# Second turn of a decode kernel: wo turned inside the norm, w1's second half turned tile by tile, last writes on two queues, the gradient row by two transposes

## The chip, the cores and the metric

The kernel runs on one core of one Trainium2 chip. TensorE is called PE, VectorE DVE, ScalarE ACT, GpSimd POOL, SyncE SP. DMAs are issued by SP (loads, and a few writes) and by POOL (most writes), and run on 16 DMA engines.

The metric is the device time of one execution in microseconds. It is compared by medians of runs; the profile is of one execution, whose own time and span are given with it. Times inside the profile count from the start of its span.

## The reference, cut to what matters

Two layers are run with the same weights, each a decode step of attention over a cache and an MLP, and then the gradients of everything:

```python
B, Sq, D = 2, 1, 1024
Hq, Hkv, Sk, Dh = 32, 4, 16384, 128        # F = 3584
x = A_x
x = x + A(layernorm(x), k_cache, v_cache, wq, wo)      # layer 0: q = x@wq, scores over 16384 keys, softmax, @v, @wo
x = x + gelu(layernorm(x) @ w1 + b1) @ w2 + b2
x = x + A(layernorm(x), k_cache, v_cache, wq, wo)      # layer 1: the same weights and the same cache
x = x + gelu(layernorm(x) @ w1 + b1) @ w2 + b2
out, vjp = jax.vjp(f, A_x, A_k_cache, A_v_cache, A_wq, A_wo, B_w1, B_b1, B_w2, B_b2)
return (out, *vjp(grad_out))
```

All arrays are bf16. out_0 is the result, [2, 1, 1024]; out_1 the gradient of x, of the same shape; out_2 and out_3 are the gradients of the two caches, as large as these (32 MB each); out_4 to out_9 those of the weights and biases.

## The kernel before, in words

**Order of the work.** The phases are: attention forward of layer 0, its MLP, attention forward of layer 1 (to about 409 us), the *second turn* (the MLP of layer 1 forward up to the gelu and, at once, its backward, 409 to 448), attention backward of layer 1 (448 to about 640), the turn of layer 0, attention backward of layer 0, in which nearly all gradients are written, and the last writes (to 1107).

Every phase is written as a list of small pieces: `emit(fn, uses)` records a function and the chunks of memory that it uses. Nothing is scheduled by the compiler: `Program.run` calls the recorded functions one after another, so that each engine's instructions have just the order in which the pieces were emitted.

**Loads.** A `Chunk` is 1 MB, [128, 4096] bf16. There are 16 slots of that size, and some more in tiles that are free for a time (two in `e1`, two in `ds1`, one in `late`). `run` hands slots to loads in the order of first use, and issues a load on SP as early in the program as a slot will come free; on the chip, SP then waits for the last reader of that slot, and everything behind that load on SP waits too. At most 8 of SP's DMAs are in flight (8 semaphores in turn). `keep` lets a chunk that is needed again later hold its slot in between, if enough slots are left, and its second load goes away. Chunks without a load (the turned tiles of w1, the row of out_0) take slots of the same stock.

**The second turn.** w1 lies in eight tiles `ws1[j]` of [128, 3584]. The forward multiplies each with the normed x (`w1_fwd`, L862: 28 matmuls for each tile). The backward needs w1 the other way round: `turn_cols` (L470 to L476) transposes a quarter of a tile (128x448 words) on DVE into a turned tile, `w1t[h][cg]`: half h (w1 tiles 4h to 4h+3), column group cg. There are 32 such turns, at L473. `turned_products` (L479, matmuls L487) multiplies a turned tile with the gradient of the gelu's input, 28 matmuls each; that needs all four w1 tiles of its half to be turned in this column group. Sums of both halves go to `sb`, and `mlp_in_bwd` copies them out (`unquad`, L517) and takes them through the norm's backward.

The norm is `ln_fwd` (L623 to L645): two sums over partitions by PE (`part_sum`, L594), between them DVE's small steps, then the power -1/2 on POOL (L642). `mlp_in` (L913) calls it and leaves the normed x in `m_all`. The gelu is `gelu` (L881); its argument `mid` is a list of pieces run in its middle, between DVE's steps, while ACT takes the exponential.

wo, too, is turned for the first kv group of the backward: `turn_here` (L446 to L461) transposes 8 blocks of 128x128 on PE (L452) and copies them back over the original on ACT (L455). `wo_first_ops` (L969) gives eight such turns.

Before the change, `w1_turn(j)` gives the four turns of tile j. Those of tile 0 run in the end of attention forward; those of tiles 1 to 5 behind that tile's products; one turn of tile 6 in the middle of the gelu, and the other three with tile 7's four behind it. All eight turned tiles have a slot of their own. wo's turns stand two behind w1's tile 5, two behind tile 6, and four in the gelu. The products of all eight turned tiles come last (L1447 to L1488).

**The row of out_0.** The result of the MLP (`xM1`, [128, 8, 2] in f32, a column layout) is ready in the backward of layer 1, at its step 26. At step 30 (L1507) `col_to_row` (L609 to L621) turns it into two rows of 1024: eight PE transposes of [128, 2] into PSUM (L617), two copies of 2x512 on DVE (L618), and a write by POOL (L619). The row stands in a chunk of kind "load", so a later load into that slot waits on SP for the write to have landed.

**The end.** `attn_bwd` for layer 0 closes with the list at L1157 to L1161: the last units of the cache gradients (`kv_units`), the gradient of x through the first norm (`parts`; its last piece calls `col_to_row` for out_1), and the units of the last weight gradient, wq's (`units`). `pieces_rows` (L1335) with `fine` writes that gradient in 256 KB pieces, one for each 128 rows, by SP (L1349).

Of the kernel before, what the change touches and what calls it, by code (L numbers as in the profile page):

```python
# [182 lines left out]
def kernel(  # L183
# [63 lines left out]
    def flat(t):  # L247
        return t.rearrange("p a b -> p (a b)")
# [360 lines left out]
    def col_to_row(colT, dram_out, queue=None, kind="half"):  # L609
        c = P.chunk(kind=kind)  # L610

        def f():
            row = c.ap[0:2, 0:D]
            for j0 in range(0, DJ, 4):
                ps = ob()[0:2, :].rearrange("p (a b) -> p a b", a=4)
                for j in range(4):
                    PE.transpose(ps[:, j, :], colT[:, j0 + j, :], identf[:])  # L617
                V.tensor_copy(out=row[:, j0 * 128:(j0 + 4) * 128], in_=flat(ps))  # L618
            (queue or GP).dma_start(dram_out, row)  # L619

        return f, [c]  # L621

    def ln_fwd(xT, name, twice=False):  # L623
        s1 = small.tile([128, 2], F32, name="ln_s1")
        V.tensor_reduce(out=s1[:], in_=xT.rearrange("p j b -> p b j"), axis=AX.X, op=ALU.add)
        ps = part_sum(s1[:], 2)
        negmu = small.tile([128, 2], F32, name="ln_negmu")
# [7 lines left out]
        ps2 = part_sum(s2[:], 2)  # L635
        vpe = small.tile([128, 2], F32, name="ln_vpe")
# [5 lines left out]
        GP.tensor_tensor(out=rstd[:], in0=vpe[:], in1=neghalf[:], op=ALU.pow)  # L642
        y = vec.tile([128, DJ, 2], F32, name=name + "_y")
# [269 lines left out]
    def mlp_in(l, xT):  # L913
        y, r = ln_fwd(xT[:], f"m{l}", twice=True)
        V.tensor_copy(out=m_all[:, :, 2 * l:2 * l + 2], in_=y[:])
        saved[f"m{l}"] = (y, r)
# [110 lines left out]
    def attn_bwd(l, order, gT, wo_first, outputs=None, mark=None, extra=None):  # L1027
# [127 lines left out]
        if l == 1:  # L1155
            todo = tail + parts
        else:  # L1157
            rows, kv_units, units = outputs(s, True)
            todo = ev.pop(s) + kv_units[0:4] + rows + kv_units[4:6] + tail[0:4] + kv_units[6:8] + tail[4:] + kv_units[8:10]
            todo += parts[0:1] + units[0:4] + parts[1:2] + units[4:8] + parts[2:3] + kv_units[10:13] + parts[3:]  # L1160
            todo += kv_units[13:] + units[8:]  # L1161
# [173 lines left out]
    def pieces_rows(out_ap, n_in, n_out, c0=0, fine=False):  # L1335
# [302 lines left out]
```

## Time and profile before

| | |
|---|---|
| runs | 1108.69, 1110.71, 1111.01 us; median 1110.71 |
| profiled execution | 1109.68 us; its span 1107.9 us; granted PE clock 0.929 |
| busy | PE 810.2 us (73%), DVE 761.4 (69%), ACT 492.3 (44%), POOL 178.5 (16%) |
| DMA | 450.03 MB, mean 406 GB/s; SP's queue (q1) 353.41 MB, POOL's (q0) 94.43 MB |
| second turn | last V load used at 409.22, m_all at 417.70, gelu from 428.64, products' copy L517 at 439.74, first turned block of the backward (L537) at 448.07 |
| SP's waits, 420 to 520 us | 14.5 for L473 (two loads), 12.4 for out_0's row (one load) |
| out_0's row | PE from 487.85, DVE to 490.41, issued 490.71, landed 495.38 |
| end | PE, DVE and ACT done at about 1097.3; last write issued 1101.01; last DMA landed 1106.6 |

How to read it: the forty slices of the page show, for each 1/40 of the span (27.7 us), the busy share of each engine in tenths and what the DMA engines moved. Groups name an instruction by its line, engine, operation and tiles (out<-in). A wait is written as the engine and what it was about to do, then what it waited for: the total in us, how often, and the longest. "SPq" is SP's queue: SP standing before the issue of a DMA. A load counts as landed when its last part has arrived; its latency holds the time behind the loads that were issued before it.

### The profile page before, as it was taken

What the parts mean: (1) busy time and instruction counts of PE and PEld (TensorE: products, weight loads), DVE (VectorE), ACT (ScalarE), POOL (GpSimd) and SP (SyncE); (2) the same over time, 40 slices, a digit from 0 to 9 for tenths busy, and PEclk for the clock granted to TensorE, in tenths of its full rate; (3) what the DMA queues carried; (4) which work ended last, traced back from release to release, by engine and by line L of the source; (5) the groups of instructions that cost most, each with busy time, mean ns of one, the idle gap of its engine ahead of it and who ended that gap; (6) DMA issues with size and microseconds to landing.
All of it is one profiled execution on the core that took longest, in us unless ns stands there. A gap on an engine that the chain in (4) does not pass through costs nothing. (4 is left out here: it accounts for less than half of the span.)

```text
span 1107.9 us, 34190 instructions
## 1 busy us (share of the span) xinstructions
PE 810.2 (73%) x14677; PEld 608.8 (55%) x14689; DVE 761.4 (69%) x1474; ACT 492.3 (44%) x1133; POOL 178.5 (16%) x571
## 2 busy tenths in 40 slices
PE   5664666457888647888678668878886987598795
PEld 4554565456777547777677565444443444344453
DVE  5864665169888627665646475979776896598984
ACT  0322223102233222235444326777675776477874
POOL 1000000001000000111111101433332332233430
PEclk9999999999999999999878657989996998799998
DMA  9999999999999998999999989999999999999996
GB/s 375 420 423 421 421 426 421 395 403 399 418 422 422 421 421 328 409 417 421 420 421 421 417 326 406 369 381 423 420 419 425 423 420 422 425 412 420 410 423 259
DMA packets 98312, 450.03 MB, mean 406 GB/s; under 512 B 7624, under 2 KB 11734, under 8 KB 59632
## 3 DMA queue, kind: packets, MB, share of 16 engines
q1 hardware_dynamic: 81232, 353.41, 78.4%
q0 software_dynamic: 16928, 94.43, 20.7%
q8 instruction: 115, 1.88, 0.6%
q14 instruction: 37, 0.30, 0.1%
HBM read 349.20 MB, written 98.62 MB: 404 GB/s over the span
## 5 line engine op out<-in xcount | busy, mean ns | idle before, releaser
L537 DVE STREAM_TRANSPOSE kT<-slot 128x512 int32<-128x512 int32 x420 | 283.2, 694 | 109.8 <-PE sc L550 89.5
L550 PE MATMUL sc<-qbd,kT 128*128 128x32 bf16 x4096 | 262.9, 223 | 11.0 <-DVE kT L537 9.7
L550 PEld LDWEIGHTS <-kT 128*128 128x128 bf16 x4096 | 209.3, 115 | 63.7 <-issue 33.6
L575 PEld LDWEIGHTS <-slot 128*128 128x128 bf16 x3520 | 144.0, 103 | 108.6 <-issue 45.0
L575 PE MATMUL sb<-xt,slot 128*128 128x8 bf16 x3520 | 161.3, 177 | 51.1 <-DMA slot<-in_A_v_cache_dram 24.5
L276 ACT CAST slot<-sc 128x512 bf16<-128x512 f32 x293 | 166.5, 594 | 57.1 <-PE sc L1321 32.6
L1261 PE MATMUL sc<-slot,late 128*128 128x512 bf16 x345 | 128.8, 393 | 19.0 <-DVE slot L279 6.5
L279 DVE CAST slot<-sc 128x512 bf16<-128x512 f32 x170 | 113.7, 677 | 25.1 <-PE sc L1261 13.4
L763 ACT ACTIVATE e<-sc 128x512 bf16<-128x512 f32 x32 | 19.0, 597 | 235.9 <-DVE sc L760 168.3
L276 ACT CAST slot<-sb 128x512 bf16<-128x512 f32 x139 | 82.4, 593 | 38.8 <-PE sb L1321 16.9
L455 ACT COPY slot<-tp 128x512 int32<-128x512 int32 x88 | 50.2, 586 | 105.5 <-PE tp L452 105.2
L452 PE MATMUL tp<-ident,slot 128*128 128x128 bf16 x768 | 71.3, 255 | 11.9 <-DMA slot<-in_A_wq_dram 6.2
L585 ACT COPY xt<-e 32x128 int32<-32x128 int32 x256 | 75.6, 295 | 3.9
L1261 PEld LDWEIGHTS <-late 128*128 128x128 bf16 x512 | 44.5, 98 | 59.6 <-issue 46.1
L1261 PE MATMUL sb<-slot,late 128*128 128x512 bf16 x161 | 63.6, 395 | 11.7 <-DVE slot L279 6.5
L1321 PE MATMUL sc<-slot,late 128*128 128x512 bf16 x157 | 60.5, 404 | 12.3 <-DVE e L279 6.9
L437 DVE STREAM_TRANSPOSE slot<-slot 128x1024 int32<-128x1024 int32 (+1 forms) x48 | 55.3, 1177 | 16.8 <-DMA slot<-in_A_wo_dram 8.5
L452 PEld LDWEIGHTS <-slot 128*128 128x128 bf16 x768 | 57.9, 116 | 14.5 <-DMA slot<-in_A_wq_dram 6.7
L279 DVE CAST slot<-sb 128x512 bf16<-128x512 f32 x82 | 55.6, 678 | 9.2 <-PE sb L1321 3.9
L642 POOL TENSOR_TENSOR m_rstd<-ln_vpe,neghalf 128x2 f32<-128x2 f32 x2 | 1.4, 717 | 352.6 <-DVE ln_vpe L640 352.6
L585 POOL COPY xt<-late 32x64 int32<-32x64 int32 x240 | 55.2, 230 | 12.9 <-DVE late L1049 2.2
L585 POOL COPY xt<-ds 32x64 int32<-32x64 int32 x128 | 29.5, 231 | 158.6 <-DVE ds L1049 115.3
(300 smaller groups left out, 1098.7 us busy)
## 6 DMA issues: line engine op xcount, KB each, us to landing
slot<-in_A_k_cache_dram SPq DMA_DIRECT2D x105, 1024.0 KB, 17.5
slot<-in_A_v_cache_dram SPq DMA_DIRECT2D x98, 1024.0 KB, 18.0
out_dram<-slot POOLq DMA_DIRECT2D x55, 1024.0 KB, 14.4
slot<-in_A_wq_dram SPq DMA_DIRECT2D x25, 1024.0 KB, 16.1
slot<-in_A_wo_dram SPq DMA_DIRECT2D x25, 1024.0 KB, 19.7
slot<-in_B_w_dram SPq DMA_DIRECT2D x23, 896.0 KB, 15.8
out_dram<-slot POOLq DMA_DIRECT2D x40, 512.0 KB, 14.3
slot<-in_B_w_dram SPq DMA_DIRECT2D x12, 1024.0 KB, 13.5
```

What stands on the lines that cost most here:

```text
L276: S.copy(out=dst, in_=src)
L279: V.tensor_copy(out=dst, in_=src)
L437: V.transpose(out=t.ap[:, h * nw * 256:(h + 1) * nw * 256].bitcast(I32).rearrange("p (w j m) -> p w j m", j=4, m=32), in_=c.ap[:, 0:4 * nc ...
L452: PE.transpose(tp[:, j * 128:(j + 1) * 128], c.ap[:, off + j * 128:off + (j + 1) * 128], ident[:])
L455: S.copy(out=d.bitcast(I32), in_=tp.bitcast(I32))
L537: V.transpose(out=kT[:].bitcast(I32).rearrange("p (w j m) -> p w j m", w=4, j=4), in_=c.ap[:, (i % 4) * 1024:(i % 4 + 1) * 1024].bitcast(I ...
L550: PE.matmul(sc[:, a0:a0 + 4, :, 2 * (i % 4) + q], lhsT=kv[:, 2 * q + w, :, e], rhs=qbd[:, q_at(g), 2 * w + e], start=(w == 0 and e == 0), ...
L575: PE.matmul(acc, lhsT=c.ap[:, n * 128:(n + 1) * 128], rhs=xv[:, i // 4, t // 2, :, 2 * (i % 4) + t % 2], start=(fresh and i == 0 and t == ...
L585: (GP.tensor_copy if on[t % len(on)] == "g" else S.copy)(out=d[32 * t:32 * t + 32, c0:c0 + cn, j, :], in_=s[32 * j:32 * j + 32, c0:c0 + cn ...
L763: S.activation(out=e_of(l, g)[:, 8 * f:8 * f + 8].rearrange("p a h b -> p h a b"), in_=sc[f][:].rearrange("p h (a b) -> p h a b", b=8), fu ...
L1261: PE.matmul(ps, lhsT=hold["blk"][:, j, :], rhs=flat(qm(w)[:, hf * 4:hf * 4 + 4, :]), start=True, stop=True)
L1321: PE.matmul(ps, lhsT=hold[j // 4 * 4][:, j % 4, :], rhs=Y.ap[:, y_at + c0:y_at + c0 + cn], start=True, stop=True)
```

## The change

Four edits, all of them of the order and form of work that stays the same otherwise.

1. The norm of the second turn takes pieces into its three gaps (`gaps`): behind the first and the second sum, and behind the power. Into these go w1 turns 2, 3 and 4 and three of wo's eight turns; the turns ahead of the norm are two and not four. Two w1 turns stand behind each of the first six w1 tiles; two w1 turns and three of wo's turns lie in the middle of the gelu.
2. w1's second half is turned by column group, not by w1 tile: turns 16 to 19 are column group 0 of tiles 4 to 7, and so on. A turned tile of this half is then complete after four turns, and its products can follow. Products of the first half and the last two wo turns lie between. The slots: the two last turned tiles of this half take the slots of two others again, once these are read.
3. `col_to_row` makes the row of [8, 2, 128] by two transposes of [128, 8] and one copy of 8x256, and writes it in 16 pieces of 128 elements, where it had two rows of 1024. This is for out_0 and out_1.
4. The end: of the last eight 256 KB writes, those with j0 < 4 are issued by POOL, the others by SP. Two units of the cache gradients move from behind the last piece of `parts` to ahead of it.

The planner's results change with this: one V chunk more keeps its slot from the forward to the backward, so SP issues one load less.

```diff
@@ col_to_row
-            row = c.ap[0:2, 0:D]
-            for j0 in range(0, DJ, 4):
-                ps = ob()[0:2, :].rearrange("p (a b) -> p a b", a=4)
-                for j in range(4):
-                    PE.transpose(ps[:, j, :], colT[:, j0 + j, :], identf[:])
-                V.tensor_copy(out=row[:, j0 * 128:(j0 + 4) * 128], in_=flat(ps))
-            (queue or GP).dma_start(dram_out, row)
+            row = c.ap[0:DJ, 0:256].rearrange("p (b n) -> p b n", b=2)
+            ps = ob()[0:DJ, 0:256].rearrange("p (b n) -> p b n", b=2)
+            for b in range(2):
+                PE.transpose(ps[:, b, :], colT[:, :, b], identf[:])
+            V.tensor_copy(out=row, in_=ps)
+            (queue or GP).dma_start(dram_out.rearrange("b (j n) -> j b n", n=128), row)
@@ ln_fwd
-    def ln_fwd(xT, name, twice=False):
+    def ln_fwd(xT, name, twice=False, gaps=((), (), ())):
...
         ps = part_sum(s1[:], 2)
+        for fn in gaps[0]:
+            fn()
...
         ps2 = part_sum(s2[:], 2)
+        for fn in gaps[1]:
+            fn()
...
         GP.tensor_tensor(out=rstd[:], in0=vpe[:], in1=neghalf[:], op=ALU.pow)
+        for fn in gaps[2]:
+            fn()
@@ attn_bwd, the end
-            todo += parts[0:1] + units[0:4] + parts[1:2] + units[4:8] + parts[2:3] + kv_units[10:13] + parts[3:]
-            todo += kv_units[13:] + units[8:]
+            todo += parts[0:1] + units[0:4] + parts[1:2] + units[4:8] + parts[2:3] + kv_units[10:15] + parts[3:]
+            todo += kv_units[15:] + units[8:]
@@ pieces_rows
-                        nc.sync.dma_start(out_ap[(j0 + j) * 128:(j0 + j + 1) * 128, c0:c0 + cn], ap[:, j * cn:(j + 1) * cn])
+                        (GP if j0 < n_in // 256 else nc.sync).dma_start(out_ap[(j0 + j) * 128:(j0 + j + 1) * 128, c0:c0 + cn], ap[:, j * cn:(j + 1) * cn])
@@ the second turn
-    def w1_turn(j, cgs=range(4)):
-        return [turn_cols(ws1[j], j % 4, w1t[j // 4][cg], cg) for cg in cgs]
+    def w1_turn(h, j, cg):
+        return turn_cols(ws1[4 * h + j], j, w1t[h][cg], cg)
+
+    w1_turns = [w1_turn(0, j, cg) for j in range(4) for cg in range(4)]
+    w1_turns += [w1_turn(1, j, cg) for cg in range(4) for j in range(4)]
...
-    xA1 = attn_fwd(1, down, lambda: xM0, mark("e1"), w1_turn(0), tw[5][1] + tw[6][0] + tw[6][1] + [(dh_last_, ())])
-    emit(lambda: mlp_in(1, xA1))
+    xA1 = attn_fwd(1, down, lambda: xM0, mark("e1"), w1_turns[0:2], tw[5][1] + tw[6][0] + tw[6][1] + [(dh_last_, ())])
...
+    gaps = [w1_turns[2:3] + wo_turns1[0:1], w1_turns[3:4] + wo_turns1[1:3], w1_turns[4:5]]
+    emit(lambda: mlp_in(1, xA1, [both(ops)[0] for ops in gaps]), both(sum(gaps, []))[1])
     for j in range(DJ):
-        for b in w1_ops[j] + (w1_turn(j) if 1 <= j < 6 else []) + wo_turns1[2 * j - 10:2 * j - 8] * (j in (5, 6)):
+        for b in w1_ops[j] + (w1_turns[5 + 2 * j:7 + 2 * j] if j < 6 else []):
             emit(*b)
...
-        gelu(1, hps1, dh, lambda: [fn() for fn, _ in w1_turn(6, (0,)) + wo_turns1[4:]])
-
-    emit(turn_round, [ws1[6], w1t[1][0]] + ws_o)
-    for cg in range(4):
-        for b in (w1_turn(6, (cg,)) if cg else []) + w1_turn(7, (cg,)):
-            emit(*b)
-    for h in range(2):
-        for cg in range(4):
-            for b in turned_products(lambda h=h: dm_1[:, h], w1t[h][cg], 14 * cg, 14, vh1, cg == 0, cg == 3):
-                emit(*b)
+        gelu(1, hps1, dh, lambda: [fn() for fn in both(w1_turns[17:19] + wo_turns1[3:6])[0]])
+
+    emit(turn_round, both(w1_turns[17:19] + wo_turns1[3:6])[1])
+    p0, p1 = [[turned_products(lambda h=h: dm_1[:, h], w1t[h][cg], 14 * cg, 14, vh1, cg == 0, cg == 3)[0] for cg in range(4)]
+              for h in range(2)]
+    for b in (w1_turns[19:20] + p0[0:1] + w1_turns[20:24] + p0[1:4] + wo_turns1[6:7] + p1[0:1] + w1_turns[24:28] +
+              wo_turns1[7:8] + p1[1:2] + w1_turns[28:32] + p1[2:4]):
+        emit(*b)
```

More of the change, by code (lines that the diff above doesn't have):

```diff
@@ L911, in gelu, with mlp_in @@
         return slope() if dh is None else None
-    def mlp_in(l, xT):
-        y, r = ln_fwd(xT[:], f"m{l}", twice=True)
+    def mlp_in(l, xT, gaps=((), (), ())):
+        y, r = ln_fwd(xT[:], f"m{l}", twice=True, gaps=gaps)
         V.tensor_copy(out=m_all[:, :, 2 * l:2 * l + 2], in_=y[:])
@@ L1448, with both @@
     w1t = [[P.chunk() for _ in range(4)] for _ in range(2)]
-    def w1_turn(j, cgs=range(4)):
-        return [turn_cols(ws1[j], j % 4, w1t[j // 4][cg], cg) for cg in cgs]
-    xA1 = attn_fwd(1, down, lambda: xM0, mark("e1"), w1_turn(0), tw[5][1] + tw[6][0] + tw[6][1] + [(dh_last_, ())])
-    emit(lambda: mlp_in(1, xA1))
+    def w1_turn(h, j, cg):
+        return turn_cols(ws1[4 * h + j], j, w1t[h][cg], cg)
+    w1_turns = [w1_turn(0, j, cg) for j in range(4) for cg in range(4)]
+    w1_turns += [w1_turn(1, j, cg) for cg in range(4) for j in range(4)]
+    def both(ops):
+        return [fn for fn, _ in ops], [c for _, us in ops for c in us]
+    xA1 = attn_fwd(1, down, lambda: xM0, mark("e1"), w1_turns[0:2], tw[5][1] + tw[6][0] + tw[6][1] + [(dh_last_, ())])
     hps1, w1_ops = w1_fwd(1, ws1)
```

## The prediction

> **What bounds the kernel now.** I read the busy shares and the forty slices first: they say which resource is full, and where it is not.
>
> ```profile
> PE 810.2 (73%) x14677; PEld 608.8 (55%) x14689; DVE 761.4 (69%) x1474; ACT 492.3 (44%) x1133; POOL 178.5 (16%) x571
> ...
> DMA  9999999999999998999999989999999999999996
> GB/s 375 420 423 421 421 426 421 395 403 399 418 422 422 421 421 328 409 417 421 420 421 421 417 326 406 369 381 423 420 419 425 423 420 422 425 412 420 410 423 259
> ```
>
> No engine reaches 75%; the transfers stand at 421 GB/s in most slices. The 450.03 MB at that rate are 1069 us of the span of 1107.9, so some 39 us are holes. Three touch the change: slice 16 (the second turn, 328 GB/s), the stretch behind it, and the last slice (259). A table by windows of 4 us (length, busy time of PE, weight loads, DVE, ACT, POOL, clock, DMA share, GB/s) shows the first hole:
>
> ```profile
> 424.00:428.00 4.00, 4.00 (x82) 4.00 (x80) 3.91 (x8) 2.21 (x4) 0.00 (x0) 1.00 0.92 317
> 428.00:432.00 4.00, 3.24 (x31) 3.08 (x30) 3.54 (x14) 1.79 (x4) 0.00 (x0) 1.00 0.94 342
> 432.00:436.00 4.00, 2.82 (x98) 2.71 (x96) 3.55 (x7) 0.58 (x1) 0.00 (x0) 1.00 0.64 263
> 436.00:440.00 4.00, 3.71 (x139) 3.62 (x136) 1.59 (x5) 0.05 (x1) 0.00 (x0) 1.00 0.52 131
> ```
>
> Against 421 GB/s these four lack 4 x (104+79+158+290)/421 = 6.0 us of transfer. The share column still reads 0.92 and 0.94 in the first two, so there some of the 16 DMA engines were late with a backlog while others ran dry; a load counts as landed with its last part. By landings the hole is smaller: the load of 428.79 lands at 436.4, the next, issued 436.93, at 442.3; that is 5.9 apart where 1 MB at 421 GB/s takes 2.45, 3.5 late. SP's waits (total, times, longest) say why no load was issued, and show a second long stop:
>
> ```profile
> SPq L378 <- DVE slot L473: 14.5, 2, 7.7
> SPq L373 <- DMA out_dram<-ds: 12.4, 1, 12.4
> ```
>
> The first is slots that w1's turns hold; the second, 483.06 to 495.40, is a load that needs the slot in which out_0's row lies until it is written. DVE's timeline of the turn (start, length, line, in brackets the idle time before):
>
> ```profile
> 422.64 6.08 DVE L473 STREAM_TRANSPOSE slot<-slot 128x448 int32<-128x448 int32 x11
> 428.64 0.17 DVE L884 TENSOR_TENSOR hpre<-sc,b1T 128x56 f32<-128x56 f32 x1
> ...
> 433.58 3.79 DVE L473 STREAM_TRANSPOSE slot<-slot 128x448 int32<-128x448 int32 x7
> 439.74 0.17 DVE L517 COPY uq<-sb 128x16 f32<-128x16 f32 x1 [2.37 <-PE sb L487]
> ```
>
> The gelu begins behind the eleven turns, although PE's last w1 product (L862) ends at 427.87. Then seven turns run beside the 224 products L487 (433.59 to 439.71), and the gradient waits for PE.
>
> **The change, part by part.**
>
> *Norm.* The norm leaves DVE idle 0.75, 0.75 and 0.84 us (L628, L637, L644). The change takes two of the four turns ahead of it away (L473, 0.55 each in a run) and puts one turn (0.60 to 0.67) into each gap, with three wo turns (8 transposes, 0.93 on PE) where PE is idle 0.95 to 2.06. Gain: 413.47 becomes 412.7; m_all 417.7 becomes 417.0 (between -1.1, two whole turns, and 0, if a gap's turn waits for its tile).
>
> *Products of w1.* They cannot end before w1's eighth tile lands: the fourth landed at 419.82, then one per 2.13 us, so 426.2; with 28 products (0.93) 427.25. The gelu gains 428.64 - 427.28 = 1.36. Two turns and three wo turns lie inside the gelu (one and two before): +0.55 on DVE. dh 431.60 becomes 431.0, the spread vector kT (ends 433.54) 432.7.
>
> *Second half, tile by tile.* Thirteen turns and two wo turns now come behind kT, where seven turns were. And the two slots of w1t[1] serve twice, so that a turn waits until PE has read the tile it overwrites. Order with row durations (28 products 0.77 to 0.89, four turns 2.2, wo turn 0.93): p0[0] to 433.7; turns 20-23 to 436.0, beside p0[1..3]; wo turn 6 to 436.7, p1[0] to 437.6; turns 24-27, which wait for it, to 439.9; wo turn 7 and p1[1] in their shadow to 439.2; p1[2] to 440.8; turns 28-31 to 442.1; p1[3] to 443.0, against 439.7. So the backward of attention starts 3.3 us later. Bounds: +1.2 if no wait binds (PE's two wo turns, 1.87, less 0.8), +4.0 if turns cost 0.67 throughout. I take the worked order.
>
> *Loads.* w1's first three tiles are turned and multiplied early, so SP issues three loads of w2 at about 418 to 422, where the second and third now go at 426.69 and 436.93. The next needs p0[1] read, 434.5, and lands 5.4 later at 439.9, 1.0 late where 3.5 was: a gain of 2.5. One load, a V chunk read again at 428.79, goes, since the chunk keeps its slot: 2.45. So the stream is some 5.0 us ahead. Bounds: 2.45 (only the load) and 8.5 (the 6.0 too).
>
> *What becomes of it.* From 444 to 490 PE waits for no load (18.85 of 20 us busy from 460 to 480), so an earlier landing moves nothing there. At 490 stands the second stop:
>
> ```profile
> 482.64 0.38 SPq L378 DMA_DIRECT2D slot<-in_A_wq_dram  x1
> 495.44 0.33 SPq L373 DMA_DIRECT2D ds<-in_A_v_cache_dram  x1
> ```
> ```profile
> 490.71 0.62 POOL L619 DMA_DIRECT2D out_dram<-ds  x1 [7.23 <-DVE ds L618]
> ```
>
> The row's write is issued 490.71 and landed 4.7 us later. The load of 482.64 landed at 498.46, so this stop just missed emptying the stream. After: compute is 3.3 later; the row's two transposes and one copy take 0.42 + 0.42 (a 128x512 copy 0.68, a 128x16 one 0.17; between them by size) where eight and two took 487.85 to 490.41, worth -1.45; so the write goes out at about 492.6. The stream, 5.0 ahead, is empty at 493.5. For the landing the bounds are 4.7, as now, and 3.0 (a load into a quiet queue, 436.93, took 5.4, less 2.45 for its 1 MB); I take 3.7, the shortest landing of any write to HBM in this trace. SP goes on at 496.3 (495.6 to 497.3) against 495.44: the lead is spent in a hole of some 5 us, and the stream behind it is 0.8 us later (+0.1 to +1.9).
>
> *Behind.* From 530 to 640 PE waits for data, and the stream stands at 419 GB/s:
>
> ```profile
> PE sb L575 <- DMA slot<-in_A_k_cache_dram: 10.2, 8, 2.7
> ```
>
> With two waits on wq (6.2 and 2.8) this makes 19 us of slack in compute, which absorbs the 1.85 us that it is late; the stream's 0.8 goes through to the end. Moving two output units ahead of out_1's row and that row's six transposes less (0.27 each) lie before 1097.3, when compute is done.
>
> *End.* The last 9 us are transfers:
>
> ```profile
> 1099.00:1100.00 1.00, 0.00 (x0) 0.00 (x0) 0.00 (x0) 0.00 (x0) 0.00 (x0) 1.00 0.07 23
> ...
> 1103.60:1106.00 2.40, 0.00 (x0) 0.00 (x0) 0.00 (x0) 0.00 (x0) 0.00 (x0) 0.50 0.07 26
> ```
>
> 26 GB/s is 421/16: one DMA engine works off a backlog, the others are done. Four of the last eight 256 KB writes (L1349) go to POOL's queue; SP's wait of 4.3 us before its writes shortens, but the backlog does not: 0. Bounds: -3.0 (1.7 us of two windows at 23 and 135 GB/s, in which SP held writes back, and 1.3 of compute) and +1.6 (four issues on POOL at 0.72 where SP's take 0.33).
>
> Sum: +0.8 + 0 = +0.8 us. On the profiled execution (1109.68; 1107.9 span and 1.8 around it) that is 1110.5; it lies 1.0 under the median of the runs, 1110.71, to which I add: 1111.5.
>
> Two rules of the Trainium skill speak against the change. Its page "DMA: Bandwidth & Descriptors", section "Specifications", says that transfers under 512 B are read, modified and written; the new rows go out in pieces of 256 B. No run here shows such a write, and by that rule the row lands nearer to 4.7 than to 3.7, which makes the sum 1112.6 at most. The section "Latency and other measured facts" of that page says that two of the DMA engines are usually slower, and guesses at a port that they share with the descriptors of GpSimd's queue. The trace agrees that one engine lags, and says nothing of why. By that guess the four writes on POOL's queue lengthen its backlog; with the +1.6 above the time would be 1113.1, and a twentieth of the chances, within the first rival's, is for that.
>
> **Rivals.**
> *Late start carried through* (slower): the backward of layer 1 is paced by compute, because SP gets slots only when PE or DVE frees them (DVE L537 12.4 us and PE L575 9.3 of SP's waits from 420 to 520). Then all 3.3 us stay: 1114.0. For it: those waits. Against: the 19 us in which PE waits for loads. It decides if these waits fall under 2 us.
> *The stop at out_0 gives way* (faster): the products of the second half hide behind the turns (+1.2), the write goes out at 490.5 (490.71 + 1.2 - 1.45) and lands in 3.0; SP issues at 493.5, 1.9 us earlier than now and as the stream empties, so that no hole opens, and 1.4 of the end's compute (six transposes of 0.27 less, one copy) shortens the last writes too: 1107.4. For it: PE and DVE could alternate there. Against: three groups of turns wait on PE.
> *Shorter end* (faster): as the sum, with the -3.0 at the end: 1108.5, at the bound of what counts as faster. For it: SP's waits of 4.3 us before its last writes. Against: the lagging engine never pauses after 1100.
>
> **How the numbers follow.** Chances: sum 0.36, late start 0.32, stop gives way 0.22, shorter end 0.10. A measurement of this kernel tells about 0.2%, 2.2 us, from no change: under 1108.5 is faster, over 1112.9 slower. The sum's spread behind the gate (+0.1 to +1.9) lies inside that, so it is the whole of "same"; faster 0.32, same 0.36, slower 0.32. The sum's own range is 1110.8 to 1112.6. With the others it is 1106.5 to 1115.0: 0.9 under the second rival (a lead of 5.8 and not 5.0) and 1.0 over the first (the start 4.0 late, and part of POOL's issues).
>
> **What would show it.** Turn: L517's copy of the products (uq) at 443 and not 440; L473 three times inside the norm; the V loads one fewer, and no 131 GB/s in 436 to 440. Gate: SP's wait for out_dram<-ds ends after 495.4, and windows from 493 to 500 fall under 300 GB/s. If that wait is gone, or ends before 493, the second rival holds; if 530 to 640 no longer shows waits for loads, the first. The prediction is wrong if the start of the first L537 of the backward lies under 1 or over 4 us later than 448.07, or if the last slice reaches over 300 GB/s.

## The result, and the profile after

| | before | after |
|---|---|---|
| median of 22 runs each | 1110.35 us | 1108.13 us |
| ratio, 95% interval | | 0.9980 (0.9974 to 0.9986): 1.6 to 2.9 us faster |
| profiled execution, span | 1109.68, 1107.9 | 1108.07, 1106.3 |
| moved | 450.03 MB | 448.98 MB |

The forecast was 0.8 us slower; the time is 2.2 us lower. The change is faster by a clear, small amount, and the prediction had the sign wrong.

The forty slices of the changed kernel, first the DMA share, then what was moved:

```profile
DMA  9999999999999999999999989999999999999996
GB/s 379 422 422 422 421 424 422 395 402 397 414 422 421 422 421 377 417 369 416 418 422 421 417 322 413 346 402 423 420 414 424 423 419 421 426 395 419 411 423 268
```

The slice of the second turn went from 328 to 377 GB/s, and two slices on there is a new hole: 369, where 417 stood. The last slice is as it was (259, now 268).

The program is the same up to the turn, yet the attention forward ended between 408.95 and 411.30 in the fourteen traces of this study. So what follows counts from L795 (the first instruction on DVE behind attention forward; L800 in the changed kernel, L794 or L801 where an experiment's edit moves the lines): 410.28 in the trace of before, 408.95 in that of after. Of the 1.6 us between the two profiled spans, 1.3 thus lie ahead of the change. DVE's timeline of the changed turn:

```profile
426.55 0.22 DVE L889 TENSOR_TENSOR hpre<-sc,b1T 128x56 f32<-128x56 f32 x1 [4.20 <-PE sc L867]
...
432.81 2.23 DVE L473 STREAM_TRANSPOSE ds<-slot 128x448 int32<-128x448 int32 x4 [0.30 <-PE sb L487]
436.65 2.22 DVE L473 STREAM_TRANSPOSE slot<-slot 128x448 int32<-128x448 int32 x4 [1.61 <-PE sb L487]
438.80 2.18 DVE L473 STREAM_TRANSPOSE ds<-slot 128x448 int32<-128x448 int32 x4
441.98 0.17 DVE L517 COPY uq<-sb 128x16 f32<-128x16 f32 x1 [1.00 <-PE sb L487]
```

DVE now stands idle for 4.20 us ahead of the gelu, and the turns of the second half wait for PE afterwards. The products' copy L517 starts 33.0 us behind L800, against 29.5 before: 3.6 us later. So the late start that was forecast is there. Windows of the changed kernel, in 4 us and then in 2 us:

```profile
424.00:428.00 4.00, 2.76 (x58) 2.68 (x56) 1.31 (x7) 0.47 (x2) 0.00 (x0) 0.50 1.04 405
428.00:432.00 4.00, 1.72 (x20) 1.29 (x18) 3.43 (x10) 1.42 (x3) 0.00 (x0) 0.50 0.98 375
432.00:436.00 4.00, 4.00 (x131) 4.00 (x130) 2.73 (x5) 0.08 (x1) 0.00 (x0) 0.50 0.72 244
436.00:440.00 4.00, 3.12 (x87) 2.94 (x84) 3.35 (x7) 1.09 (x2) 0.00 (x0) 0.50 1.01 420
...
490.00:492.00 2.00, 2.00 (x35) 1.90 (x33) 1.50 (x3) 0.01 (x1) 0.68 (x1) 0.50 0.69 261
492.00:494.00 2.00, 2.00 (x63) 2.00 (x61) 1.45 (x4) 0.61 (x2) 0.00 (x0) 0.83 0.27 41
494.00:496.00 2.00, 1.24 (x40) 1.05 (x37) 2.00 (x4) 1.78 (x7) 1.07 (x5) 1.00 0.81 279
```

The hole of the turn is about half as large as it was (counted below), and the hole at out_0's row, which the prediction put at some 5 us, is there too, with 3.8 us. What differs is its end. SP's issues and POOL's write of the row in the changed kernel:

```profile
484.62 0.38 SPq L378 DMA_DIRECT2D slot<-in_A_wq_dram  x1
492.94 0.33 SPq L373 DMA_DIRECT2D ds<-in_A_v_cache_dram  x1
```
```profile
491.20 0.68 POOL L618 DMA_DIRECT2D out_dram<-ds  x1 [5.73 <-DVE ds L617]
```

From POOL's issue to SP's next load there are 1.74 us. In the kernel before there were 4.73 (490.71 to 495.44); the prediction took 3.7 for the landing and 3.0 as its lower end.

To compare traces, two numbers are worked out from windows of each: the hole of the turn (10 to 40 us behind L795/L800, 30 us long) and the hole behind it (40 to 120, 80 us), each as its length times (1 - GB/s / 421). Before: 327 and 418 GB/s, 6.7 and 0.6 us. After: 378 and 401, 3.1 and 3.8.

Where the gain lies can be read from two rows of DVE in each trace: the one that the count starts from, and the last write of `dq_all`, with which the attention backward of layer 1 ends. Before, then after:

```profile
410.28 0.17 DVE L795 TENSOR_TENSOR oT<-sb,rbc 128x8 f32<-128x8 f32 x1 [13.72 <-PE sb L575]
642.18 0.18 DVE L1056 TENSOR_SCALAR dq_all<-sb 128x8 bf16<-128x8 f32 x1 [1.36 <-PE sb L575]
```
```profile
408.95 0.17 DVE L800 TENSOR_TENSOR oT<-sb,rbc 128x8 f32<-128x8 f32 x1 [12.70 <-PE sb L575]
639.43 0.17 DVE L1061 TENSOR_SCALAR dq_all<-sb 128x8 bf16<-128x8 f32 x1 [1.34 <-PE sb L575]
```

Between the two lie 231.9 us before and 230.5 after, 1.4 less. The experiments below give more such traces. The four with the old turn have 231.9 to 232.5 (mean 232.2), the six with the new turn, the new row and a load that waits for it 229.7 to 230.6 (mean 230.3). From there to the end of the span all ten take 465.3 to 467.3, and both groups have the mean 466.2. So the whole gain of about 2 us is there when this phase ends, and in these traces nothing is added behind it.

### The profile page after: what moved, and what is told of

It is laid out like the page before. It is cut to its first block, busy times and chain, and to the rows that moved or that the text cites. A ratio compares the mean times of both kernels' runs of the same rounds, so it can differ in the third digit from the quotient of the medians.

```text
span 1106.3 us, 34160 instructions
## 1 busy us (share of the span) xinstructions
PE 808.9 (73%) x14665; PEld 608.4 (55%) x14677; DVE 760.4 (69%) x1472; ACT 492.9 (45%) x1133; POOL 181.7 (16%) x575
## 2 busy tenths in 40 slices
DMA packets 97932, 448.98 MB, mean 406 GB/s; under 512 B 7624, under 2 KB 11742, under 8 KB 59380
## 5 line engine op out<-in xcount | busy, mean ns | idle before, releaser
L537 DVE STREAM_TRANSPOSE kT<-slot 128x512 int32<-128x512 int32 x420 | 283.2, 694 | 107.5 <-PE sc L550 88.3
L550 PE MATMUL sc<-qbd,kT 128*128 128x32 bf16 x4096 | 262.9, 222 | 10.8 <-DVE kT L537 9.8
L550 PEld LDWEIGHTS <-kT 128*128 128x128 bf16 x4096 | 209.5, 116 | 60.8 <-issue 30.3
L575 PEld LDWEIGHTS <-slot 128*128 128x128 bf16 x3520 | 143.9, 103 | 110.5 <-issue 48.8
L575 PE MATMUL sb<-xt,slot 128*128 128x8 bf16 x3520 | 161.2, 176 | 50.8 <-DMA slot<-in_A_v_cache_dram 24.1
L276 ACT CAST slot<-sc 128x512 bf16<-128x512 f32 x281 | 160.8, 593 | 61.3 <-PE sc L1266 25.5
L276 ACT CAST slot<-sb 128x512 bf16<-128x512 f32 x151 | 89.5, 593 | 36.4 <-PE sb L1326 24.9
L585 ACT COPY xt<-e 32x128 int32<-32x128 int32 x256 | 75.7, 296 | 3.9
L585 POOL COPY xt<-late 32x64 int32<-32x64 int32 x240 | 55.6, 232 | 12.8 <-DVE late L1054 1.7
L585 POOL COPY xt<-ds 32x64 int32<-32x64 int32 x128 | 29.7, 232 | 155.1 <-DVE ds L1054 103.6
## 6 DMA issues: line engine op xcount, KB each, us to landing
slot<-in_B_w_dram SPq DMA_DIRECT2D x12, 1024.0 KB, 13.6
```

The costliest lines, as they stand in the source:

```text
L276: S.copy(out=dst, in_=src)
L537: V.transpose(out=kT[:].bitcast(I32).rearrange("p (w j m) -> p w j m", w=4, j=4), in_=c.ap[:, (i % 4) * 1024:(i % 4 + 1) * 1024].bitcast(I ...
L550: PE.matmul(sc[:, a0:a0 + 4, :, 2 * (i % 4) + q], lhsT=kv[:, 2 * q + w, :, e], rhs=qbd[:, q_at(g), 2 * w + e], start=(w == 0 and e == 0), ...
L575: PE.matmul(acc, lhsT=c.ap[:, n * 128:(n + 1) * 128], rhs=xv[:, i // 4, t // 2, :, 2 * (i % 4) + t % 2], start=(fresh and i == 0 and t == ...
L585: (GP.tensor_copy if on[t % len(on)] == "g" else S.copy)(out=d[32 * t:32 * t + 32, c0:c0 + cn, j, :], in_=s[32 * j:32 * j + 32, c0:c0 + cn ...
```

## The experiments

Each ran in five rounds beside the kernel before. The table has all of them, with the kernel before and the changed one; "row", "SP on" and "dq_all" are POOL's issue of out_0's row, SP's next load and the end of layer 1's attention backward, in us behind L795/L800, and "wait" is what lies between the first two. The ratio comes from all runs, the other columns from one trace each.

| kernel | ratio (95%) | hole of the turn | hole behind | row | SP on | wait | dq_all |
|---|---|---|---|---|---|---|---|
| before | 1 | 6.7 | 0.6 | 80.4 | 85.2 | 4.73 | 231.9 |
| e2_row | 1.0001 (0.9992 to 1.0010) | 6.2 | 0.2 | 77.1 | 82.1 | 5.03 | 232.2 |
| e3_tail | 0.9996 (0.9987 to 1.0006) | 6.3 | 0.4 | 80.5 | 85.3 | 4.81 | 232.3 |
| e9_before_keep | 0.9999 (0.9991 to 1.0008) | 9.6 | 0.4 | 80.5 | 85.3 | 4.87 | 232.5 |
| e1_turn | 0.9992 (0.9983 to 1.0001) | 3.1 | 5.9 | 83.5 | 85.2 | 1.71 | 232.8 |
| e4_turn_tail | 0.9996 (0.9987 to 1.0006) | 2.9 | 5.7 | 83.5 | 85.3 | 1.72 | 232.1 |
| after | 0.9980 (0.9974 to 0.9986) | 3.1 | 3.8 | 82.3 | 84.0 | 1.74 | 230.5 |
| e6_after_again | 0.9984 (0.9975 to 0.9994) | 3.6 | 4.2 | 82.6 | 84.4 | 1.74 | 230.6 |
| e8_old_end | 0.9982 (0.9972 to 0.9991) | 2.9 | 4.0 | 82.1 | 83.8 | 1.75 | 229.7 |
| e7_reread | 0.9987 (0.9978 to 0.9996) | 3.8 | 4.2 | 82.3 | 84.0 | 1.74 | 230.4 |
| e12_after_keep | 0.9982 (0.9974 to 0.9991) | 7.2 | 3.8 | 82.0 | 83.9 | 1.91 | 230.1 |
| e11_fill5 | 0.9982 (0.9973 to 0.9990) | 6.7 | 1.7 | 79.2 | 83.9 | 4.68 | 230.5 |
| e5_after_own | 0.9984 (0.9975 to 0.9992) | 2.9 | 4.9 | 85.6 | 82.0 | none | 231.6 |
| e13_fill5_own | 0.9988 (0.9979 to 0.9997) | 7.1 | 0.2 | 84.6 | 81.0 | none | 231.3 |

### e1_turn: the turn alone

The changed kernel, with `col_to_row` and the end as they were:

```diff
-            row = c.ap[0:DJ, 0:256].rearrange("p (b n) -> p b n", b=2)
...
+            row = c.ap[0:2, 0:D]
+            for j0 in range(0, DJ, 4):
...
-                        (GP if j0 < n_in // 256 else nc.sync).dma_start(out_ap[(j0 + j) * 128:(j0 + j + 1) * 128, c0:c0 + cn], ap[:, j * cn:(j + 1) * cn])
+                        nc.sync.dma_start(out_ap[(j0 + j) * 128:(j0 + j + 1) * 128, c0:c0 + cn], ap[:, j * cn:(j + 1) * cn])
...
-            todo += kv_units[15:] + units[8:]
+            todo += kv_units[13:] + units[8:]
```

> The second turn alone (gaps of the norm, second half by column group, one V load less); the old row of out_0 (eight transposes, two copies, two pieces of 2 KB) and the old end. Theory A, the gate: the lead of the loads is spent at the row of out_0, and the new form of the row is what let the write land 1.7 us after its issue. With the old row SP goes on 1.5 us later for the longer making of the row, and up to 3 us more for the landing: 1.5 to 4.5 us later than in the changed kernel, so 0 to 3 us slower than the kernel before. Theory B, the loads: the row's form does not matter and the turn itself gains; then 1 to 2 us faster than before, and the row's write again lands in under 2.5 us.

Measured: 0.9992 (0.9983 to 1.0001), 0.9 us faster at the middle, not clear of none. The row is issued 1.3 us later than in the changed kernel, and lands after 1.71 us although its form is the old one:

```profile
493.24 0.62 POOL L619 DMA_DIRECT2D out_dram<-ds  x1 [6.82 <-DVE ds L618]
```
```profile
494.96 0.33 SPq L373 DMA_DIRECT2D ds<-in_A_v_cache_dram  x1
```

So the first half of theory A falls: the short landing does not come with the new form. Theory B has its second sign, a landing under 2.5 us, but falls in its size: the turn alone doesn't bring 1 to 2 us with certainty, and in its trace `dq_all` comes no sooner than in the kernel before (232.8). What stays is that SP goes on 85.2 us behind L800, as in the kernel before, with a hole of 5.9 us.

### e2_row: the row alone

The kernel before with the new `col_to_row` and nothing else.

> The kernel before with the new row alone (out_0 and out_1 by two transposes, one copy, 16 pieces of 256 B). Theory A: POOL issues the write 1.4 us sooner and it lands in about 2 us, where 4.7 were; SP goes on at about 491 to 492 and not 495.4. The stream has a backlog until 498.5 there, so nothing is gained but a few tenths: within 1 us of before. If the short landing belongs to the empty queue and not to the form of the row, the landing stays at 4 to 5 us.

Measured: 1.0001 (0.9992 to 1.0010), no gain. POOL's issue and SP's next load:

```profile
487.88 0.68 POOL L618 DMA_DIRECT2D out_dram<-ds  x1 [5.73 <-DVE ds L617]
```
```profile
492.91 0.33 SPq L373 DMA_DIRECT2D ds<-in_A_v_cache_dram  x1
```

The row is 3.3 us earlier. Of this the new form makes 1.5 (from the `dq_all` of DVE just ahead of the row to POOL's issue it takes 2.4 us, where it took 3.9); the other 1.8 were there ahead of the row, at POOL's copies L585, and nothing in this edit explains them. The wait is 5.03: the new form lands no sooner than the old one (4.73 to 4.87 in three traces) while loads are under way (the window of 490 to 492 moved 435 GB/s). With e1_turn this is the pair that settles it: the landing goes by what is in the DMA queues, 1.7 us when the loads are running dry and 4.7 to 5.0 when not, and not by whether the row goes out in two pieces or sixteen. SP went on 3.0 us earlier and nothing came of it, because the stream had its backlog there: the last load issued ahead of the row landed at 500.91, 8.0 us behind SP's next issue. The limit was the transfers ahead of it, not SP.

### e3_tail and e8_old_end: the end

e3_tail is the kernel before with the new end; e8_old_end is the changed kernel with the old end.

```diff
-                        nc.sync.dma_start(out_ap[(j0 + j) * 128:(j0 + j + 1) * 128, c0:c0 + cn], ap[:, j * cn:(j + 1) * cn])
+                        (GP if j0 < n_in // 256 else nc.sync).dma_start(out_ap[(j0 + j) * 128:(j0 + j + 1) * 128, c0:c0 + cn], ap[:, j * cn:(j + 1) * cn])
```

> The kernel before with the new end alone (four of the last 256 KB writes on POOL's queue, two cache units ahead of out_1's row). Theory C, the end: the last part of the trace is 1.4 us shorter in the changed kernel, and this edit makes it: 1.4 us faster than before, the last writes issued by about 1098.5 and not 1101. By the recorded sum, nothing: the engine that lags has the same backlog, so 0.

> The changed kernel with the old end (all last writes on SP, the two cache units behind out_1's row). The new end alone gave 0.4 us (-0.6 to 1.4) in the kernel before. If the parts add, 0.4 us slower than the changed kernel. If the new end needs the short row of out_1 ahead of it, as the two profiles suggest (from the last compute to the end of the span 10.8 us before and 9.4 after, but 10.6 with the new end alone), 1.4 us slower.

Measured: 0.9996 (0.9987 to 1.0006) and 0.9982 (0.9972 to 0.9991), the latter as the changed kernel in the same rounds (0.9984). SP's last issues in e3_tail and, with the old end, in e8_old_end:

```profile
1097.10 1.14 SPq L1349 DMA_DIRECT2D out_dram<-slot  x2
1098.34 1.11 SPq L1349 DMA_DIRECT2D out_dram<-ds  x2
```
```profile
1095.92 2.49 SPq L1354 DMA_DIRECT2D out_dram<-slot  x2
1098.62 0.95 SPq L1354 DMA_DIRECT2D out_dram<-ds  x2
```

With the new end the last write went out 1.9 us behind the first of these four, with the old one 3.3; and the time does not show it. The end is worth nothing that five rounds can tell, in either kernel. Theory C, which was formed from one pair of profiles, is not borne out.

### e6_after_again: the changed kernel once more

> The changed kernel itself, once more, beside the next three, so that these can be read against it in the same rounds and a second profile shows what of the first is chance: 2.2 us faster than before (1.6 to 2.9). In its trace, the hole of the second turn again 3 us smaller than in the kernel before, and again a hole of about 3 us at out_0's row.

Measured: 0.9984 (0.9975 to 0.9994). Its trace has both holes again (3.6 and 4.2 us) and a wait of 1.74.

### e4_turn_tail: the changed kernel with the old row

```diff
-            for b in range(2):
-                PE.transpose(ps[:, b, :], colT[:, :, b], identf[:])
-            V.tensor_copy(out=row, in_=ps)
...
+                for j in range(4):
+                    PE.transpose(ps[:, j, :], colT[:, j0 + j, :], identf[:])
+                V.tensor_copy(out=row[:, j0 * 128:(j0 + 4) * 128], in_=flat(ps))
```

> The changed kernel with the old row (eight transposes, two copies, two pieces of 2 KB) for out_0 and out_1. Theory A: SP goes on 1.5 to 2 us later at out_0's row, the queue being dry, and this goes through to the end: 1.5 to 2 us slower than the changed kernel; the write lands 1.7 us after its issue all the same. Theory B: the row's form does not matter: as the changed kernel.

Measured: 0.9996 (0.9987 to 1.0006), 0.4 us faster than before, where the changed kernel in the same rounds was 1.8 faster. At the middles the row makes some 1.3 us here, with intervals that overlap; it makes nothing in the kernel before (e2_row). SP goes on at 85.3, the hole behind the turn is 5.7 us where the changed kernel has 3.8 and 4.2, and `dq_all` comes at 232.1, as in the kernel before, where the changed kernel has 230.5 and 230.6.

### e7_reread: the V chunk read again

```diff
-            if a.last < b.first and all(room[i] > 0 for i in span):
+            if b.key != ("V", 0, 3) and a.last < b.first and all(room[i] > 0 for i in span):
```

> The changed kernel, but the planner may not keep the one V chunk (batch 0, head 0, last quarter), so it is loaded again in the turn as in the kernel before: 1 MB more. Theory A, the stop at out_0's row: the stream runs dry there for 3.4 us in any case, so this load, 2.5 us, fills the hole; SP goes on when the row has landed, 1.7 us after its issue in a dry queue and up to 4.7 in a full one; so 0 to 2 us slower than the changed kernel, and the hole of 490 to 496 shrinks to about 1 us. Theory D, the bytes: the gain of the change is the 1 MB that is not read; then 2.5 us slower than the changed kernel and as the kernel before, with the hole at the row as large as it was.

Measured: 0.9987 (0.9978 to 0.9996). The experiment failed in its aim: the planner used the room for a chunk of wo, so 448.98 MB were moved as in the changed kernel, and the load only changed its place. The hole behind the turn did not fill (4.2 us), and SP goes on at 84.0. It tells nothing on theory D.

### e9_before_keep: the same chunk kept in the kernel before

```diff
-SPARE = (3, 4)
+SPARE = (3, 3)
```

> The kernel before, with the planner's reserve of slots one smaller from the late attention forward on (SPARE 3, 3), and nothing else: this keeps the same V chunk that the changed kernel keeps, so 1 MB is not read again. Theory D, the bytes alone: 2.5 us faster than before. Theory A: the load lay in the hole of the second turn, and the slot that holds the chunk delays a load of w2 to 426.7; the hole of the turn grows by the 2.45 us that the load took (from 6.3 to 8.7), so the time stays within 0.5 us of before. Then the load counts only together with the slots that the new order of the turns frees.

Measured: 0.9999 (0.9991 to 1.0008). 1 MB less is moved, and the time stays. One window of the turn, where the kernel before has 131 GB/s, and w2's loads, of which the second and third go out at 426.9 and 429.0, the fourth at 437.1:

```profile
436.00:440.00 4.00, 3.92 (x147) 3.83 (x144) 1.63 (x5) 0.00 (x0) 0.00 (x0) 0.50 0.34 121
```

The hole of the turn is 9.6 us where it was 6.2 to 6.7: it grew by 2.9 to 3.4, more than the 2.5 us that the load had taken. Theory D in its plain form is out: a load that is not read is worth nothing where the stream has a hole in any case.

### e12_after_keep: one chunk more kept in the changed kernel

The same line in the changed kernel; the planner keeps a chunk of wo, and 447.93 MB are moved.

> The changed kernel with the planner's reserve one smaller (SPARE 3, 3): one chunk of wo more is kept, 1 MB less is read, in the stretch from 560 to 700 us where the transfers are full. If a load that is not read counts where the stream is full and the slot is not missed, 2.5 us faster than the changed kernel, 4 to 5 us faster than before. If the slot is missed, the stretch from 560 to 700 shows a hole of its own and the gain is under 1 us.

Measured: 0.9982 (0.9974 to 0.9991), as the changed kernel. The hole is in the turn, not between 560 and 700 where it was expected: 7.2 us and not 3.1, because the slot is missed there by w2. SP goes on at 83.9, as in the changed kernel.

### e5_after_own: no load waits for the row

```diff
-        c = P.chunk(kind=kind)
+        c = P.chunk(kind=kind) if kind is not None else None
...
-            row = c.ap[0:DJ, 0:256].rearrange("p (b n) -> p b n", b=2)
+            row = (c.ap[0:DJ, 0:256].rearrange("p (b n) -> p b n", b=2) if c is not None else vh1()[0:DJ].rearrange("p w a n -> p (w a n)")[:, 0:256].rearrange("p (b n) -> p b n", b=2))
...
-    extra[30] = [col_to_row(xM1, out_0.rearrange("b s d -> (b s) d"), kind="load")]
+    extra[30] = [col_to_row(xM1, out_0.rearrange("b s d -> (b s) d"), kind=None)]
```

> The changed kernel with out_0's row in a tile of its own that no load uses (the spread vector's, unused since the second turn), so no load waits for the write. The stream then has no hole from 490 to 496 (261, 41 and 279 GB/s there lack 3.2 us). Theory A: the stream sets the end of the backward of layer 1, so up to 3.2 us faster than the changed kernel, 4 to 5 us faster than before. Rival: the backward of layer 1 is paced by compute, and the hole costs nothing; then as the changed kernel, 2.2 us faster than before, and PE waits for K loads less between 530 and 640 with the same end.

Measured: 0.9984 (0.9975 to 0.9992), as the changed kernel. The wait for the row is gone, and SP's waits between 420 and 520 are for slots that compute frees:

```profile
SPq L373 <- DVE kT L537: 28.7, 9, 5.0
SPq L373 <- PE sb L575: 9.8, 5, 3.6
SPq L373 <- PE sb L487: 8.7, 2, 8.4
SPq L378 <- DVE kT L537: 7.9, 2, 4.6
```

In the changed kernel the first of these is 24.8 us, the last 3.4, and the row's wait 7.9. The hole is 4.9 us all the same; only its cause has another name.

But this edit does more than take the wait away. The row's new tile, `vh1`, is one of the three buffers of the pool `ktp`, into which DVE turns the K chunks (`kT`, L537), and it is now held until the row is written. The waits of L537 for PE, in 52 us from 35.1 behind L800, in the changed kernel and here:

```profile
DVE kT L537 <- PE sc L550: 9.7, 10, 2.1
```
```profile
DVE kT L537 <- PE sc L550: 16.2, 15, 2.1
```

The row is issued 3.3 us later than in the changed kernel. So a gain from the missing wait can be hidden by what the missing buffer costs, and the run doesn't tell what the wait itself is worth.

### e11_fill5 and e13_fill5_own: the products earlier

e11_fill5 takes most of the late start back; e13_fill5_own is that with the row of e5_after_own.

```diff
+        tile_turns = {4: w1_turns[13:17], 5: w1_turns[17:18] + wo_turns1[6:7], 6: w1_turns[18:19] + wo_turns1[7:8], 7: []}
-        for b in w1_ops[j] + (w1_turns[5 + 2 * j:7 + 2 * j] if j < 6 else []):
+        for b in w1_ops[j] + (w1_turns[5 + 2 * j:7 + 2 * j] if j < 4 else tile_turns[j]):
...
-        gelu(1, hps1, dh, lambda: [fn() for fn in both(w1_turns[17:19] + wo_turns1[3:6])[0]])
+        gelu(1, hps1, dh, lambda: [fn() for fn in both(wo_turns1[3:6])[0]])
...
-    for b in (w1_turns[19:20] + p0[0:1] + w1_turns[20:24] + p0[1:4] + wo_turns1[6:7] + p1[0:1] + w1_turns[24:28] +
-              wo_turns1[7:8] + p1[1:2] + w1_turns[28:32] + p1[2:4]):
+    for b in (w1_turns[19:20] + p0[0:1] + w1_turns[20:24] + p0[1:2] + w1_turns[24:28] + p0[2:3] + w1_turns[28:32] + p0[3:4] + p1):
```

> The changed kernel with the late start taken back in part: w1 turns 17 and 18 in DVE's idle time ahead of the gelu, wo turns 6 and 7 in PE's idle time between w1's tiles, and the turned tiles of the second half in the slots of the first half's one after the other, so that no turn waits behind the products of its own half. The products should end 2.5 to 3 us earlier than in the changed kernel. Theory A: out_0's row is earlier by as much, and its hole shrinks from 3.5 to about 1 us; but w1's last tiles and the first half's slots come free later, which costs the turn up to 3 us of transfer; so between 2.5 us faster and 0.5 slower than the changed kernel. Rival, the late start does not matter at all: the row's hole stays as it is.

Measured: 0.9982 (0.9973 to 0.9990), as the changed kernel, within the range given and at no gain. The copy L517 starts 29.8 us behind L800, 3.2 earlier, and the row is issued at 79.2, 3.0 earlier. Yet SP goes on at the same place, 83.9:

```profile
490.27 0.68 POOL L618 DMA_DIRECT2D out_dram<-ds  x1 [5.72 <-DVE ds L617]
```
```profile
494.95 0.33 SPq L373 DMA_DIRECT2D ds<-in_A_v_cache_dram  x1
```

The earlier row finds loads under way and needs 4.68 us to land; 3.0 us are won in compute and 2.9 of them lost in the landing. And the turn has its old hole again, 6.7 us, since w1's last tiles come free later: "SPq L373 <- DVE slot L473" is 11.8 us, its longest 11.6.

> The kernel with the earlier products (e11_fill5), and out_0's row in a tile of its own as in e5_after_own, so that no load waits for its write. Theory A in its present form: what fixes the end of this stretch is when SP goes on with loads at this place, 84.0 us after the end of attention forward in all kernels with the new row and 85.2 with the old one, whatever was read less or earlier ahead of it. Without the row's write SP goes on when PE has read the K chunk in that slot, about 80 us after; the stream still has a backlog of 2 us there, so its hole behind the turn falls from 1.8 us to about 0.5: 1 to 1.5 us faster than e11_fill5, 3 to 3.5 us faster than before. Rival: as in e5_after_own the loads behind then wait for their own slots, and the time stays 2 us under before.

Measured: 0.9988 (0.9979 to 0.9997), no faster than e11_fill5. SP goes on at 81.0 and the hole behind the turn is closed (0.2 us), as theory A had it, but the time doesn't follow; the two loads behind it wait for slots that DVE's L537 and PE's L575 read. The time fits the rival. Yet the buffer of `kT` is missing here too: L537 waits 17.1 us for PE where e11_fill5 has 9.5, and the row is issued 5.4 us later than there. So the run can't tell the rival from this loss, and whether the end of the stretch hangs on the wait for the row alone stays undecided.

No version beat the changed kernel.

## Why the prediction was wrong, step by step

All measured times are behind L795/L800 and set back to the frame of the trace of before (410.28).

- **Norm.** m_all by 0.7 earlier was forecast; 0.83 measured (415.54 - 408.95 against 417.70 - 410.28). Right.
- **w1's products and gelu.** 1.36 forecast, 0.76 measured. PE's products of the eighth tile began when it had landed, as the step had it, but at 425.61, 16.7 us behind L800, where the forecast's 426.2 is 15.9 behind L795. The tile whose landing at 419.82 the step starts from is w1's fifth, not the fourth; with three more at 2.13 us its sum comes out as it stands.
- **Second half.** ("Tile by tile" there means one turned tile after the other.) 3.3 us later forecast (1.2 to 4.0), 3.6 measured. Right, and for the reason given: the turns wait for PE.
- **Loads.** Three loads of w2 at 418 to 422 were forecast; they went out at 418.1, 418.9 and 424.0. The loads at 426.69 and 436.93 in the kernel before are w2's third and fourth; the second, at 413.50, was overlooked, and goes out 4.6 us later now. The next load, when p0[1] is read: forecast 434.5, measured 433.55, which is 434.9 in that frame. One load less. That some DMA engines were dry while others were late at 424 to 432 is not shown: the share there, 0.92 and 0.94, is a mean over all 16. The stream was to be empty at 493.5; the load of 484.62 landed at 492.64, that is 494.0. Right to half a microsecond.
- **The row.** Issue forecast at 492.6; measured 491.20, that is 492.5. The shorter making was put at 1.45 and measured 1.5 (from the `dq_all` just ahead of it to the issue, 3.9 before and 2.4 after). Right.
- **The landing: here the prediction failed.** It took 3.7 us, with 3.0 and 4.7 as ends. The wait was 1.74. All three came from the wrong rows. 4.7 is the landing beside loads, 3.7 that of a larger write elsewhere in the trace (512 KB, issued at 698.88), and 3.0 what a load of 1 MB left over its time at full rate, longer than the whole landing of a write of 4 KB. In the twelve traces with the wait, it is 1.71 to 1.91 in the seven whose loads were running dry, and 4.68 to 5.03 in the five where loads were under way. Dry means here that the last load ahead of the row landed 0.2 to 1.8 us before the row did (in six; in e12_after_keep its landing is not on record); in the five it landed 2.3 to 8.1 behind. The two kernels in which no load waits for the row agree: 2.9 us in e5_after_own, where the window of 496 to 498 fell to 256 GB/s, and 4.9 in e13_fill5_own, where it moved 434. So SP went on at 494.3 and not 496.3.
- **Behind.** The stream was to be 0.8 us later than before. With 1.74 in place of 3.7 that step gives 1.2 us earlier. Measured, on two loads whose landings the DMA issues give: the K chunk into the slot "late", issued at 495.86 before and 493.37 after, took 8.4 and 8.1 us and so landed 94.0 us behind L795 and 92.5 behind L800, 1.5 earlier; the K chunk into "ds" (506.77 and 508.32, 17.9 and 13.6 us) landed at 114.4 and 113.0, 1.4 earlier. At `dq_all` it is 1.4 in this pair and 1.95 between the means of the two groups. So the step's sign turned with the landing, and 1.2 of about 2 us follow from it; the runs don't show what makes the other 0.8.
- **End.** 0 forecast, 0 measured (e8_old_end against e6_after_again). The two bounds were not needed: neither two queues nor POOL's issues can be seen in the time.
- **The range** of 1106.5 to 1115.0 held the 1108.13.

The rivals: the late start is there and was not carried through: from 530 to 640 PE still waits for K loads, as the rival's own test asked (before, the same row gives 10.2, 8, 2.7).

```profile
PE sb L575 <- DMA slot<-in_A_k_cache_dram: 11.6, 8, 3.4
```

"The stop at out_0 gives way" had the right sign and the wrong mechanism: it wanted the products hidden, and they were 3.6 us late; what gave way was the landing. By the prediction's own sign for it SP's wait was to end before 493: it ended at 492.9 in this trace, but that is 494.2 in the frame of before. "Shorter end", at 3.0 us, is refuted by e8_old_end.

How the parts make the 2.2 us, as far as the runs show it: the turn alone makes 0.9 by time (0.1 slower to 1.9 faster) and nothing by the traces up to `dq_all` (232.8 and 232.1 in the two kernels with the old row), the row alone nothing, the end nothing, and turn and row together 2.0 (e8_old_end). That is no contradiction. The turn closes 3.6 us of its hole (6.7 to 3.1 in the table) and saves one load of 2.5, and a stop at the row that SP can't pass before compute has made it takes most of that; the shorter row, worth about 1.3 us there by time and 2.1 by `dq_all`, is only of use where the stream runs dry. In holes and bytes: after, e6_after_again and e8_old_end have 6.9 to 7.8 us in the two holes together, before, e2_row and e3_tail 6.4 to 7.3, and the former move 1.05 MB less, 2.5 us: 2.0 in sum. For e1_turn and e4_turn_tail (8.6 and 9.0) it gives 0.5, measured 0.9 and 0.4. For e11_fill5 and e12_after_keep the same sum gives about 1 us less gain than measured, so it is a ledger and not a law.

What stays open: what the wait for the row is worth by itself. In the two kernels without it DVE has one buffer of `kT` less and compute is later, so they don't answer this; the row in a tile outside that pool would, and was not run.

On the rules that were weighed. The section "Specifications" of the Trainium skill's page "DMA: Bandwidth & Descriptors" would have made the 256-byte pieces slow; here the row of sixteen pieces took 1.74 us against 1.71 and 1.72 for two pieces of 2 KB, and 5.03 against 4.73 to 4.87 beside loads, so the piece decides nothing at this size. The guess on the slower engines in the section "Latency and other measured facts" of that page of the Trainium skill would have lengthened the end; e8_old_end and e6_after_again show no difference. A rule that I had not weighed would have put the landing right: the section "Anatomy of one DMA — SWDGE (gpsimd) path" of that page of the Trainium skill fits a DMA from GpSimd's queue as 2.0 us and its bytes at 436 GB/s, most of the 2 us being the receipt of the write, which gives an estimate of 2.0 us for 4 KB. The seven waits behind a dry stream, 1.71 to 1.91 us, come near it; the five beside loads, 4.68 to 5.03, lie 2.7 to 3.0 above it, so here the fit comes near for a quiet queue alone.

## What to carry to other kernels

When a change makes a queue run dry, take the latencies of a dry queue for what happens there: a small write that a load waits for took 4.7 to 5.0 us beside loads and 1.7 us without, so the hole that it makes ends itself sooner than the full queue's row says. And count what is saved ahead of such a stop only up to the stop: 2.5 us of transfer saved in a stretch that has a hole in any case were worth nothing (e9_before_keep), and 3 us of compute were eaten by a longer landing (e11_fill5).

## What the runs showed of the hardware

The landing of a 4 KB write depended on the loads under way and not on its form (above). And the granted PE clock of whole executions did not go with their time: among the 22 runs of the changed kernel, seven with a mean clock of 0.724 to 0.729 took 1106.43 to 1108.93 us, and three with 0.901 to 0.932 took 1107.85 to 1108.61. The two profiled executions had 0.929 (before) and 0.726 (after), and PE's matmuls L550 took 223 and 222 ns in them.
